# One of a unit's three weight transfers issued by ScalarE instead of SP in the first 24 slots

## The chip, the cores and the metric

The kernel runs on one core of a Trainium2 chip. The core has TensorE (PE; its weight loads are shown as PEld), VectorE (DVE), ScalarE (ACT), GpSimd (POOL) and SyncE (SP). DMAs are issued by an engine's own instruction queue, here SP's and ScalarE's, and carried by 16 DMA engines. The metric is the device time of one execution in microseconds; less is better.

## The reference

An attention block with a threshold, then a feed-forward block with SoLU and a layer norm. All data are float32, except that the weights of the second block arrive as float64.

```python
# q, k, v: (8 batches, 8 heads, 576 rows, 64), tau = 0.02
scores = (q @ k.T) / 8
scores = where(scores >= max(scores) - tau, scores, -1e9)
attn = exp(scores - max(scores))
attn = attn / (sum(attn) + 1e-9)
x = (attn @ v)                      # to (4608 tokens, 512)

h = x @ w_in                        # 512 -> 1024
sm = softmax(h)
solu = h * sm
ln = (solu - mean) / sqrt(var + 1e-6) * g_ln
out = ln @ w_out                    # 1024 -> 512
```

## The kernel before

**Slots and units.** The attention is cut into 144 slots, 18 for each of the 8 batches. A slot is 128 rows of scores for each of two heads. In a batch, 16 slots are of kind 0 or 1 (the first 512 of the 576 rows, four pairs of heads) and the last two of kind 2 (the last 64 rows). Two slots in a row, r = 0 and r = 1, make a unit. So units of kind 0 and 1 end at the odd slots 1, 3, ... 15, then 19, 21, ... 33, and so on; slot 17 ends a unit of kind 2.

**What happens to a slot.** The outer loop counts rounds (`rnd`); each round begins one slot. `scores` (L434) multiplies queries and keys on TensorE into two PSUM tiles. `maxes` (L455) takes the row's extreme on VectorE. `ramp` (L470) and `exps` (L479) run on ScalarE, two instructions each. A round later `normalise` (L486, L487, L489) scales the weights `w` on GpSimd, and `blocks` (L501) transposes them on VectorE in blocks of 32 by 32 into the tile T. T holds both slots of a unit, and there are two T buffers.

**The step that the change touches.** The block transposes leave each block at its own 32 partitions. After the second slot of a unit, three DMAs carry T into the tile wT (two buffers), in which the 576 key rows stand on two halves of 64 partitions: one of 576 KB from T's partitions 32 to 95 (L510), and two of 288 KB from partitions 0 to 31 and 96 to 127 (L512). All three are issued by SP, in this order. Units of kind 2 use four smaller ones (L517).

**Who uses wT.** `attend_steps` (L542), three or four rounds after the unit's second slot, multiplies wT with the values on TensorE into pv. Its first instructions read the lower 64 partitions, its later ones the upper. `attended` (L572) copies pv to xh on ScalarE. When the four units of one kind of a batch are done, their tokens go through the feed-forward block: `ff_h` (L605, L595), `ff_max` (L620), `ff_exp` (L629), `ff_mul` (L635), `ff_stats` (L650 to L661), `ff_norm` (L671), `ff_norm2` (L676), `ff_swap` (L687, four DMAs from SP), `ff_turn` (L697), `ff_o` (L710), `ff_out` (L725) and `ff_store` (L738, two DMAs from SP).

**What else runs in the first slots.** In rounds 0 to about 15 the float64 weights are turned into float32, one piece of 128 by 512 a round. SP loads a piece (L251, 512 KB). ScalarE (L263), VectorE (L282, L286, L308) and GpSimd (L332) convert it; pieces of w_out are also scaled by ScalarE (L340). For every other piece of w_out two DMAs from SP (L347, `w<-w`, the tile w2) swap its halves. SP also loads v (L151) and the queries and keys of the next batch (L142, later L168), which TensorE turns (L379) and ScalarE or VectorE copies (L388, L390, L392).

**The order.** The schedule is written by hand: on every engine the instructions stand in the order in which the Python code records them, round after round. In round s + 1, ScalarE's queue has the ramps and exps of slot s + 1, then the copy L572 where a unit is due, and then what `blocks(s)` records for it; after that come `ff_exp`, the weight steps and the next round. Completion of DMAs is counted on eight semaphores, which the DMAs take in turn; a DMA's issue waits until the last one on its semaphore has landed.

Of the kernel before, what the change touches and what calls it, by code (L numbers as in the profile page):

```python
# [20 lines left out]
def kernel(  # L21
# [27 lines left out]
    nc = tc.nc  # L49
# [443 lines left out]
    def blocks(s):  # L493
        b, kind, hp, r = slots[s]
        key = (b, kind, hp)
        if r == 0:
            units[key] = dict(T=work.tile([P, NB, 2, 2, 32], F32, tag="T", name="T"))
        u = units[key]
        T = u["T"]
        for h, w in enumerate(live.pop(s)["w"]):  # L500
            nc.vector.transpose(out=T[:, :, r, h, :], in_=w)  # L501
        if r == 0:
            return


        T = T.rearrange("p (c m) r h x -> p c (m r h x)", c=2)
        u["wT"] = wT = work.tile([P, 2, NK, 2, 2, 32], F32, tag="wT", bufs=2, name="wT")
        to = wT.rearrange("p g m r h x -> p g (m r h x)")
        if kind < 2:
            nc.sync.dma_start(out=to[:, 1], in_=T[32:96])  # L510
            for half in range(2):
                nc.sync.dma_start(out=to[ROWS[half], 0], in_=T[96 * half : 96 * half + 32])  # L512
            return
        for g in range(2):
            for half in range(2):
                of = 64 * half + 32 * g
                nc.sync.dma_start(out=to[ROWS[half], g], in_=T[of : of + 32])  # L517
# [291 lines left out]
    with tc.manual_schedule():  # L809
# [45 lines left out]
        while True:  # L855
# [133 lines left out]
            if rnd - 1 in live:  # L989
                blocks(rnd - 1)  # L990
# [62 lines left out]
```

## Time and profile before

| | us |
|---|---|
| time, median of 3 runs | 857.37 |
| lowest and highest of the 3 | 852.65, 860.28 |
| span of the profiled execution | 854.9 |
| TensorE busy in it | 819.9 |
| VectorE, ScalarE, GpSimd busy | 674.6, 570.0, 496.1 |

The three runs are other executions than the profiled one, whose span, from the first to the last instruction, lies between the lowest and the median of them.

How rows of a timeline read: start in us, length in us, engine, line, operation, out<-in, how many were merged, and in brackets how long the engine was idle ahead of it and what ended that. SPq and ACTq are the instruction queues of SP and ScalarE: a row of theirs is the issuing of a DMA, and the transfer itself lands later. The name `w` stands for three tiles in the profile, since buffer numbers are left out: the attention weights w, and the feed-forward weights w1 and w2.

### The profile page before, as it was taken

Reading aid. Unit: us, or ns where it says so; the run is one execution under the profiler, and the core shown is the slowest. Engines: PE = TensorE matmul, PEld = TensorE weight load, DVE = VectorE, ACT = ScalarE, POOL = GpSimd, SP = SyncE. Lnnn points to the kernel's source line nnn. Section 1 sums busy time; section 2 is a strip of 40 time slices with the busy share of each in tenths; the row PEclk is TensorE's granted clock in tenths of the full one; section 3 lists DMA queues with packets and bytes.
Section 4 is the critical chain, followed back from the end, with each engine's and each line's share of the span. In section 5 each row is a group of like instructions: output and inputs, shape, how many; then the busy total and the mean of one; then the engine's idle time right before and its main releaser. Section 6 shows DMA issues by size and latency. Waiting matters only on the chain.

```text
span 854.9 us, 36109 instructions
## 1 busy us (share of the span) xinstructions
PE 819.9 (96%) x15363; PEld 620.5 (73%) x15363; DVE 674.6 (79%) x1225; ACT 570.0 (67%) x1127; POOL 496.1 (58%) x945
## 2 busy tenths in 40 slices
PE   6778899999999999999999999999999999999997
PEld 5555677778677787777688877777777777777655
DVE  5997787989788888888788878888888878787361
ACT  6886876777767666667666666666677777775121
POOL 4885656666566656565566666565666655555120
PEclk8899999999999999999999999999999999999999
DMA  9999778798888888887888778887788887655212
GB/s 343 254 249 213 191 194 233 188 259 204 226 229 202 211 185 218 216 216 190 201 215 218 195 177 209 207 217 207 195 221 226 207 188 175 165 137 140 67 38 63
DMA packets 75314, 168.54 MB, mean 197 GB/s; under 512 B 11146, under 2 KB 32658, under 8 KB 75154
## 3 DMA queue, kind: packets, MB, share of 16 engines
q1 hardware_dynamic: 74866, 165.82, 76.7%
q8 instruction: 120, 1.97, 1.0%
q10 hardware_dynamic: 288, 0.43, 0.2%
q14 instruction: 40, 0.33, 0.1%
HBM read 46.14 MB, written 9.44 MB: 65 GB/s over the span
## 4 chain that ended last, share of the span: by engine, by line
PE 83%; DMA 4%; DVE 4%; ACT 3%; issue 2%; POOL 2%; SPq 1%; DVEq 0%; ACTq 0%; POOLq 0%
PE o_ps L710 27%; PE h_ps L605 22%; PE s_ps L434 15%; PE pv L542 14%; DMA wT<-T 3%; PE h_ps L595 3%; ACT w L470 1%; DVE w L455 1%; ACT w L479 1%; DVE T L501 1%; POOL w L489 1%; POOL sm L487 0%; PE s_ps L379 0%; DVE w L308 0%; PE tp L371 0%
## 5 line engine op out<-in xcount | busy, mean ns | idle before, releaser
L710 PE MATMUL o_ps<-w,uT 64*64 64x256 f32 x4608 | 269.5, 376 | 2.2 <-issue 1.6
L470 ACT ACTIVATE w<-s_ps,nth 128x576 f32<-128x576 f32 x280 | 196.8, 738 | 105.6 <-DVE nth L455 88.6
L455 DVE CUSTOM_DVE_ANT_0 w<-s_ps,tau_t 128x576 f32<-128x576 f32 x280 | 200.0, 751 | 83.5 <-PE s_ps L434 52.4
L710 PEld LDWEIGHTS o_ps<-w,uT 64*64 64x64 f32 x4608 | 221.8, 133 | 55.4 <-ACT xh L572 12.0
L489 POOL TENSOR_SCALAR w<-w,sm 128x576 f32<-128x576 f32 x288 | 220.6, 778 | 14.3
L501 DVE STREAM_TRANSPOSE T<-w 128x576 f32<-128x576 f32 x288 | 207.7, 756 | 22.6 <-POOL w L489 22.3
L605 PE MATMUL h_ps<-w,xh 64*64 64x512 f32 x1856 | 220.8, 589 | 0.0
L479 ACT ACTIVATE w<-w,ntau 128x576 f32<-128x576 f32 x288 | 219.6, 767 | 0.0
L542 PEld LDWEIGHTS pv<-wT,v 64*64 64x64 f32 x5760 | 172.6, 136 | 39.8 <-issue 16.7
L434 PE MATMUL s_ps<-kT,qT 64*64 64x512 f32 (+1 forms) x2048 | 175.8, 416 | 13.4 <-ACT w L470 11.3
L542 PE MATMUL pv<-wT,v 64*64 64x128 f32 (+1 forms) x5760 | 173.9, 263 | 8.3 <-DMA wT<-T 7.4
L605 PEld LDWEIGHTS h_ps<-w,xh 64*64 64x64 f32 x1856 | 118.4, 133 | 77.2 <-issue 43.6
L486 POOL TENSOR_SCALAR sm<-sm 128x2 f32<-128x2 f32 x144 | 34.2, 237 | 186.5 <-ACT w L479 182.8
L487 POOL TENSOR_TENSOR sm<-sm,mone 128x2 f32<-128x2 f32 x144 | 106.7, 741 | 12.0
L434 PEld LDWEIGHTS s_ps<-kT,qT 64*64 64x64 f32 x2048 | 72.7, 137 | 21.7 <-ACT w L470 16.2
L572 ACT COPY xh<-pv 128x256 f32<-128x256 f32 x64 | 25.4, 396 | 80.9 <-PE pv L542 80.9
L671 ACT ACTIVATE V<-u,nb,rs 128x1024 f32<-128x1024 f32 x36 | 44.7, 1240 | 40.5 <-POOL nb L661 33.6
L697 DVE STREAM_TRANSPOSE uT<-V 128x1024 f32<-128x1024 f32 x36 | 44.1, 1225 | 15.9 <-DMA V<-u 15.6
L479 ACT ACTIVATION_READ_ACCUMULATOR w<-w,ntau 128x1 f32 x288 | 55.4, 192 | 0.0
L676 DVE TENSOR_SCALAR u<-u,rs,nb 128x1024 f32<-128x1024 f32 x36 | 34.9, 971 | 19.5 <-ACT V L671 17.9
L635 DVE TENSOR_TENSOR u<-h_ps,u 128x1024 f32<-128x1024 f32 x36 | 42.8, 1190 | 9.4 <-ACT u L629 9.4
L620 DVE TENSOR_REDUCE hm<-h_ps 128x1 f32<-128x1024 f32 x36 | 42.9, 1193 | 4.9 <-PE h_ps L595 2.7
(77 smaller groups left out, 553.5 us busy)
## 6 DMA issues: line engine op xcount, KB each, us to landing
wT<-T SPq DMA_DIRECT2D x160, 288.0 KB, 6.5
wT<-T SPq DMA_DIRECT2D x64, 576.0 KB, 5.5
v<-in_v_dram SPq DMA_DIRECT2D x16, 576.0 KB, 6.0
V<-u SPq DMA_DIRECT2D x144, 64.0 KB, 3.5
out_dram<-ob SPq DMA_DIRECT2D x71, 128.0 KB, 2.6
q<-in_q_dram SPq DMA_DIRECT2D x28, 288.0 KB, 6.1
k<-in_k_dram SPq DMA_DIRECT2D x27, 288.0 KB, 6.4
qT<-flip SPq DMA_DIRECT2D x48, 144.0 KB, 3.2
```

The source lines that it names most:

```text
L434: nc.tensor.matmul(out=ps[h][ROWS[y], ks], lhsT=lhsT, rhs=d["kT"][ROWS[h], ks], start=True, stop=True,)
L455: nc.vector.tensor_tensor_reduce(out=w, in0=ps[:, 0:S], in1=(zero if loose else tau_t).to_broadcast([P, S]), scale=1.0, scalar=BIG, op0=AL ...
L470: nc.scalar.activation(out=d["w"][x], in_=d["w"][x] if d["loose"] else d["ps"][x][:, 0:S], func=AF.Prelu, bias=d["nth"][x], scale=-1.0, al ...
L479: nc.scalar.activation(out=w, in_=w, func=AF.Exp, bias=ntau, scale=1.0, accum_out=sm[:, x : x + 1])
L487: nc.gpsimd.tensor_tensor(out=sm, in0=sm, in1=mone, op=ALU.pow)
L489: nc.gpsimd.tensor_scalar(out=w, in0=w, scalar1=sm[:, x : x + 1], scalar2=1.0, op0=ALU.mult, op1=ALU.mult)
L501: nc.vector.transpose(out=T[:, :, r, h, :], in_=w)
L542: nc.tensor.matmul(out=to, lhsT=d["v"][ROWS[u], (h0 + h - u) % 4, m,], rhs=rhs, start=m == 0, stop=m == NK - 1,)
L605: mm = nc.tensor.matmul(out=h[ROWS[y], f], lhsT=x[ROWS[r], c, ROWS[y]], rhs=w1_parts[ROWS[r], c, part ^ r], start=part == 0 and c == 0, st ...
L671: nc.scalar.activation(out=V, in_=u, func=AF.Identity, bias=nb, scale=rs)
L697: nc.vector.transpose(out=uT, in_=d["V"].rearrange("p y (m x) -> p m y x", x=32))
L710: nc.tensor.matmul(out=d["o"][ROWS[z], 512 * (r ^ other) : 512 * (r ^ other) + 256], lhsT=d["uT"][ROWS[r], m].rearrange("p y x -> p (y x)" ...
```

## The change

One line in `blocks`: for units whose second slot is below 24, the first of the three transfers is issued by ScalarE on its own queue.

```diff
         if kind < 2:
-            nc.sync.dma_start(out=to[:, 1], in_=T[32:96])
+            (nc.scalar if s < 24 else nc.sync).dma_start(out=to[:, 1], in_=T[32:96])
             for half in range(2):
                 nc.sync.dma_start(out=to[ROWS[half], 0], in_=T[96 * half : 96 * half + 32])
             return
```

That is 11 units: those of slots 1, 3, 5, 7, 9, 11, 13, 15, 19, 21 and 23. The other 53 units of these kinds, and those of kind 2, stay as they were. The turn in which DMAs take the eight semaphores changes with it. In order of instructions, ScalarE's issue stands directly behind the two exps of the following slot (slots 5, 7, 13, 19 and 21 of those), behind copies of queries and keys (slots 1 and 3), or behind the copy L572 (slots 9, 11, 15 and 23). In the first slots the weight step L263 follows it, otherwise L340, L629 or the next ramp.

## The prediction

> **What bounds the kernel now.** I read the page first: busy shares by engine and by slice.
>
> ```profile
> PE 819.9 (96%) x15363; PEld 620.5 (73%) x15363; DVE 674.6 (79%) x1225; ACT 570.0 (67%) x1127; POOL 496.1 (58%) x945
> ...
> PE   6778899999999999999999999999999999999997
> ...
> DMA  9999778798888888887888778887788887655212
> ```
>
> TensorE is full everywhere but in the first slices, and a slice is 854.9 / 40 = 21.4 us. The change ends at slot 23, so I cut the span by stages (columns: stretch, its length, busy us and instructions of PE, PEld, DVE, ACT, POOL, granted clock, DMA share, GB/s).
>
> ```profile
> 55.00:60.00 5.00, 2.19 (x52) 1.36 (x48) 4.83 (x10) 4.98 (x12) 4.65 (x8) 1.00 0.85 227
> ...
> 65.00:70.00 5.00, 4.86 (x54) 2.70 (x45) 4.33 (x10) 4.76 (x10) 4.20 (x8) 1.00 1.04 213
> 70.00:75.00 5.00, 1.84 (x40) 1.60 (x44) 3.44 (x4) 0.12 (x2) 4.36 (x7) 0.92 1.06 228
> ...
> 180.00:400.00 220.00, 219.53 (x4232) 168.21 (x4228) 185.23 (x336) 153.90 (x306) 135.87 (x263) 1.00 0.85 213
> ```
>
> From 180 us on TensorE idles 0.47 us in 220: nothing to be won or lost there unless something new breaks it. From 65 to 75 us the 16 DMA engines are at 1.04 and 1.06 of their time, and TensorE is busy 1.84 of the 5 us from 70 on. Next I read the chain of waits in order of time (start, us, what) and then TensorE's and VectorE's timelines at the same place, for what each idle gap ended on.
>
> ```profile
> 58.08 1.51 DVE T L501 x2
> ...
> 61.22 12.33 DMA wT<-T
> ```
>
> ```profile
> 57.71 0.44 PE L542 MATMUL pv<-wT,v 64*64 64x128 f32 x4 [2.10 <-DMA wT<-T]
> ...
> 72.10 0.44 PE L542 MATMUL pv<-wT,v 64*64 64x128 f32 x4 [2.24 <-DMA wT<-T]
> 73.59 3.36 PE L542 MATMUL pv<-wT,v 64*64 64x128 f32 x66 [1.06 <-DMA wT<-T]
> ```
>
> ```profile
> 78.37 0.76 DVE L455 CUSTOM_DVE_ANT_0 w<-s_ps,tau_t 128x576 f32<-128x576 f32 x1 [4.86 <-PE s_ps L434]
> ```
>
> The longest piece of the chain before the full stretch is one unit's wT, the unit of slot 9 (I count units from 0, so it is unit 4): its T is complete at 58.08 + 1.51 = 59.59, and its last half is there at about 73.55. TensorE loses 2.24 + 1.06 = 3.30 us there and VectorE 4.86. Unit 3 costs TensorE 2.10 at 57.71, beside VectorE's full 4.83 of 5 us. So 3.3 us, at most VectorE's 4.86, is what this change can win at the main place. That is under 1% (8.6 us), about what a measurement here can tell from no change: the three runs alone spread over 7.6 us.
>
> **What SP does with the three transfers.** First the sizes, from the page's list of DMA issues (KB each, median us to landing), then SP's timeline for units 3 and 4 (start, time on the queue), the two half-block issues of unit 3 by themselves (shortest, median, longest ns), and from SP's list of waits what L347 waited for (us in total, times, longest).
>
> ```profile
> wT<-T SPq DMA_DIRECT2D x160, 288.0 KB, 6.5
> wT<-T SPq DMA_DIRECT2D x64, 576.0 KB, 5.5
> ```
>
> ```profile
> 50.40 0.58 SPq L510 DMA_DIRECT2D wT<-T  x1
> 51.03 4.00 SPq L512 DMA_DIRECT2D wT<-T  x2
> 55.12 1.81 SPq L251 DMA_DIRECT2D raw<-in_moe_w_out_dram  x2
> 57.35 1.31 SPq L347 DMA_DIRECT2D w<-w  x2
> 59.64 0.58 SPq L510 DMA_DIRECT2D wT<-T  x1
> ...
> 70.75 1.98 SPq L347 DMA_DIRECT2D w<-w  x2
> ```
>
> ```profile
> L512 SPq DMA_DIRECT2D wT<-T x2: 598/1972/3345, 51.0 to 51.7; - x2
> ```
>
> ```profile
> SPq L347 <- ACT w L340: 4.2, 3, 3.6
> ...
> SPq L347 <- DMA wT<-T: 2.4, 2, 1.7
> ```
>
> The first issue of a unit takes 0.58 us, the second 0.60, the third 3.35: SP is held there, and the weight loads (L251) behind it start only at 55.12. The change takes the large first transfer (576 KB; the halves are 288 KB) off this queue. Both halves move up 0.58 + 0.05 us. If the third issue is held because the large one is in front of it, SP also wins 3.35 - 0.60 = 2.75 us, and L251 would start at about 51.7 instead of 55.12. The w swaps (L347) do not follow: they wait for ScalarE's L340 anyway. What the early weight loads buy is the unused part of 55 to 60, (1 - 0.85) x 5 = 0.75 us of all DMA engines, and perhaps as much again from what the tail behind it no longer drags. I take 1.5 us earlier for unit 4's last half (72.0 instead of 73.5), between 0 (the engines are full, the same bytes must go through) and 3.3 (all of TensorE's hole). A loss is possible too, down to the 1.5 us by which ScalarE issues unit 4's transfer later (below). The Trainium skill, DMA: Bandwidth & Descriptors, section "Issuing engines are not separate DMA queues", says that DMAs from all issuing engines run on the same 16 DMA engines, and that issuing from several saves only the time to initiate, usually small beside the transfer. By that rule alone the gain would be the 0.58 us per unit; the trace agrees on the full engines (1.04 and 1.06) and not on "small", with 3.35 us of issue in one place.
>
> **What ScalarE pays.** The issue takes about 0.6 us of its queue, 11 times (slots 1 to 15, 19, 21, 23). It stands behind the next slot's ramp (L470) and exp (L479), so it can go out later than on SP, and whatever follows on ScalarE (weight step L263 or L340, then the next ramp, which TensorE's next scores and GpSimd's next normalise wait for) is held while it waits. Does 0.6 us cost anything? ScalarE's queue works ahead of its engine:
>
> ```profile
> L263 ACTq EVENT_SEMAPHORE  x1: 17/17/17, 23.1 to 23.1; - x1
> L263 ACT ACTIVATE em<-raw x1: 679/679/679, 24.1 to 24.1; 128x512 int32<-128x512 uint32 x1
> ```
>
> ```profile
> 25.03 1.42 ACT L470 ACTIVATE w<-s_ps,nth 128x576 f32<-128x576 f32 x2 [0.20 <-DVE nth L455]
> ...
> 43.78 1.42 ACT L470 ACTIVATE w<-s_ps,nth 128x576 f32<-128x576 f32 x2 [1.64 <-DVE nth L455]
> ```
>
> The queue handled L263's wait at 23.1 while its engine came to L263 at 24.1, one microsecond later, and it is just there, ahead of L263, that unit 0's issue is put. So 0.6 us is covered by what the engine still has to do. On top there is idle time before the ramps, 0.20 us here and 1.64 in another round. I take 0 for ten of the issues; without that cover it would be 11 x 0.6 = 6.6 us less the idle time.
>
> Unit 4 is later: its place is behind the copy L572, which itself waits for unit 3's attention.
>
> ```profile
> 61.09 0.41 ACT L572 COPY xh<-pv 128x256 f32<-128x256 f32 x1 [0.83 <-PE pv L542]
> ```
>
> So it goes out at about 61.1, 1.5 us after 59.64. It does not come last for that: on a queue of its own it has nothing in front of it, while the halves stand behind two weight loads and two w swaps.
>
> **Unit 5 is the one that costs.** Each DMA of the program takes the next of eight completion semaphores, and its issue waits until the DMA eight before it has landed (that is why SP's L347, which neither reads nor writes wT, waited twice for a wT in the list of waits above). In the changed program ScalarE's transfer of unit 5 (slot 11) shares its semaphore with the first of the two w swaps that SP issues at 70.75 now, and that swap shares one with a half of unit 4. The swap's own issue and landing, and ScalarE's timeline around it:
>
> ```profile
> L347 SPq DMA_DIRECT2D w<-w x1: 653/653/653, 70.7 to 70.7; - x1
> ...
> DMA to landing us min/median/max: 8.1/8.1/8.1
> ```
>
> ```profile
> 77.20 0.39 ACT L572 COPY xh<-pv 128x256 f32<-128x256 f32 x1 [7.09 <-PE pv L542]
> 77.48 1.12 ACT L629 ACTIVATE u<-h_ps,hm 128x1024 f32<-128x1024 f32 x1
> ...
> 79.75 1.37 ACT L470 ACTIVATE w<-s_ps,nth 128x576 f32<-128x576 f32 x2
> ```
>
> It lands at 70.7 + 8.1 = 78.8. ScalarE reaches the new issue behind L572, at 77.3 now, and L629 and the ramp at 79.75 stand behind it. With everything 1.5 us earlier the swap lands at 77.3; then L629 starts at 77.3 + 0.6 = 77.9 instead of 77.48, and the ramp ends at 79.75 + 1.37 + 0.4 = 81.5 instead of 81.1. TensorE, 1.5 us ahead by then, meets that ramp at its next scores and gives back about 1 of its 1.5 us. No other unit meets such a pair: by the program's list of waits, their semaphores were last used by transfers long landed.
>
> **The sum:** SP's relief -1.5, ten hidden issues 0, the hold at unit 5 +1.0: -0.5 us. On the profiled span that is 854.4. The runs' median is 2.5 us above that span (857.37 to 854.9), so 856.9 us.
>
> **The rivals.**
> First, no gain in DMA (15 in 100). The bytes ahead of unit 4's last half are the same and the engines are full, so it lands at 73.5 still, the swap at 78.8, and ScalarE is held from 77.3 to 78.8 plus 0.6 of issue: L629 2.0 us late, of which TensorE sees about 1. Time 858.5. For it speaks the DMA share of 1.04 and 1.06; against it SP's 3.35 us hold and the 0.85 of 55 to 60. In this case the change does not do what moving a transfer seems to promise, since the halves still come last.
>
> Second, the gain is kept (20 in 100). If unit 4's halves land by 70, the swap lands by 75.5, before ScalarE comes to it; TensorE's hole of 3.3 us closes, VectorE's 4.86 with it, and unit 3's hole gives some tenths. -3.3 to -4.9, so 852.5 to 854. For it: two queues with mixed traffic may use the engines better than one. Against it: at 65 to 70 they moved only 213 GB/s at a share of 1.04, so each transfer is slow for another reason than the queue.
>
> Third, slower (15 in 100): ScalarE's issue is held as SP's third one is, because the two halves go out just ahead of it. Price: 2.5 to 3.35 us per issue, of which 1.0 is covered by the queue's lead and 0.20 to 1.64 by idle time. For the five units up to 60 us, on the chain that ends in unit 4's T, that is 5 x (2.9 - 1.0 - 0.6) = 6.5 us, and units 7 and on add up to 1.5. Time 862 to 866. It decides from an issue of 1.0 + 0.6 = 1.6 us on. The trace has just one pair issued by both engines at once:
>
> ```profile
> 851.22 0.72 ACTq L738 DMA_DIRECT2D out_dram<-ob  x1
> ```
>
> ```profile
> 851.22 0.59 SPq L738 DMA_DIRECT2D out_dram<-ob  x1
> ```
>
> ScalarE's took 0.13 us longer than SP's, which speaks against a hold, though neither had a large one beside it. The same page of the Trainium skill, section "Queues, rings and completion order", says that SP and ACT each own a ring on every DMA engine but no descriptor generator of their own; were that what holds SP's third issue, this rival follows, and the pair of 0.72 and 0.59 does not show it.
>
> **How the numbers follow.** The forecast, -0.5 with 50 in 100, has its own range of -2 to +2, so 855 to 859. The rivals give 858.5, 853 and 864. The median of a few runs moves by some 3 us by itself. Leaving out the ends of the second and third case, 8 in 10 lie in 850 to 864. Faster by over 1% (under 848.8) needs more than every wT hole together, so only the scatter of runs could show it: 0.03. Slower by over 1% (over 865.9) is the upper end of the third rival, or several holds like unit 5's that I did not see: 0.09. Within 1%: 0.88.
>
> **What would show it.** SP's third issue of a unit (now the second half) at 0.6 us and L251 of unit 3 near 51.7: relief right. ScalarE's L510 at 0.6 us with no later ramp: hidden. ScalarE idle ahead of L629 in unit 5, ended by the landing of w<-w: the hold. TensorE's two wT holes at 72 and 73.6 smaller by 1.5 in sum, and the stretch from 180 us on as long as before. The forecast is wrong if ScalarE's issues take over 1.6 us, if a wT hole turns up at a unit that has none now, or if the stretch behind 180 us changes.

## The result, and the profile after

| | median us | runs | lowest to highest |
|---|---|---|---|
| before | 855.06 | 20 | 852.48 to 861.56 |
| after | 861.11 | 20 | 855.80 to 865.07 |

The ratio is 1.0053, 95% interval 1.0029 to 1.0076: about 4.5 us of 855.06 lost (the two medians lie 6.05 us apart, the two means 4.70). The forecast was a gain of 0.5 us and a time of 855 to 859 us. The profiled execution after has a span of 857.8 us.

In what follows a hole is a stretch in which TensorE is idle, and the head is the first 85 us or so, in which the DMA engines are nearly always busy and units 0 to 5 are moved.

The same stages as before (stretch, its length, busy us and instructions of PE, PEld, DVE, ACT, POOL, granted clock, DMA share, GB/s):

```profile
50.00:55.00 5.00, 2.52 (x32) 1.43 (x28) 4.51 (x10) 4.39 (x11) 4.40 (x7) 0.56 1.04 238
55.00:60.00 5.00, 3.76 (x72) 2.87 (x64) 3.11 (x7) 2.85 (x7) 4.18 (x8) 0.76 1.03 263
60.00:65.00 5.00, 0.89 (x8) 0.52 (x12) 2.93 (x7) 2.44 (x6) 2.42 (x5) 0.58 1.04 260
...
70.00:75.00 5.00, 5.00 (x58) 3.21 (x54) 4.81 (x12) 4.91 (x10) 1.89 (x5) 1.00 0.87 218
180.00:400.00 220.00, 217.99 (x4144) 162.14 (x4140) 182.74 (x335) 152.85 (x303) 134.09 (x260) 1.00 0.84 210
```

TensorE, which idled from 70 to 75 before, is full there now. The idle stretch has moved forward: 0.89 us of work between 60 and 65, at a granted clock of 0.58. The DMA engines are full in these 15 us (1.03 to 1.04). The stretch from 180 on idles 2.01 us instead of 0.47. SP's, TensorE's and ScalarE's timelines after show what moved:

```profile
50.31 1.72 SPq L512 DMA_DIRECT2D wT<-T  x2
52.68 3.10 SPq L251 DMA_DIRECT2D raw<-in_moe_w_out_dram  x2
```

```profile
52.71 0.69 PE L542 MATMUL pv<-wT,v 64*64 64x128 f32 x4 [1.95 <-DMA wT<-T]
53.92 3.75 PE L542 MATMUL pv<-wT,v 64*64 64x128 f32 x66 [0.52 <-DMA wT<-T]
...
63.73 0.69 PE L542 MATMUL pv<-wT,v 64*64 64x128 f32 x4 [4.98 <-DMA wT<-T]
64.80 3.44 PE L542 MATMUL pv<-wT,v 64*64 64x128 f32 x66 [0.38 <-DMA wT<-T]
...
76.79 2.23 PE L542 MATMUL pv<-wT,v 64*64 64x128 f32 x70
```

```profile
68.39 0.39 ACT L572 COPY xh<-pv 128x256 f32<-128x256 f32 x1 [5.96 <-PE pv L542]
68.55 0.55 ACTq L510 DMA_DIRECT2D wT<-T  x1
...
79.31 0.55 ACTq L510 DMA_DIRECT2D wT<-T  x1
79.91 1.11 ACT L629 ACTIVATE u<-h_ps,hm 128x1024 f32<-128x1024 f32 x1 [0.34 <-issue]
```

SP is relieved: its two half-block issues take 0.54 us each, and L251 starts at 52.68 instead of 55.12. But unit 3's halves now take over 13 us to land; of the two, the profile before shows the landing of the second alone, 7.14 us after its issue (SP's L512 issues of unit 3 by themselves, shortest, median, longest):

```profile
DMA to landing us min/median/max: 13.1/13.2/13.3
```

So the holes are at units 2 (1.95 + 0.52) and 3 (4.98 + 0.38), and unit 4 has none. The page's list of DMA issues has the large transfers at 5.4 us to landing on SP's queue and 8.3 on ScalarE's (median). These are not the same transfers: the eleven are issued in the first 150 us, the 53 behind them. On SP, in both profiles of the kernel before, the eleven have a median of 6.7 us (landings are known for five and six of them, for eight on ScalarE). So the queue accounts for some 1.6 us of the difference, and the place for the rest.

```profile
wT<-T SPq DMA_DIRECT2D x53, 576.0 KB, 5.4
...
wT<-T ACTq DMA_DIRECT2D x11, 576.0 KB, 8.3
```

### The profile page after: what moved, and what is told of

Read it like the earlier page. It is cut to its first block, busy times and chain, and to the rows that moved or that the text cites. A ratio compares the mean times of both kernels' runs of the same rounds, so it can differ in the third digit from the quotient of the medians.

```text
span 857.8 us, 36130 instructions
## 1 busy us (share of the span) xinstructions
PE 819.2 (95%) x15363; PEld 617.1 (72%) x15363; DVE 674.6 (79%) x1225; ACT 570.5 (67%) x1127; POOL 494.3 (58%) x945
## 4 chain that ended last, share of the span: by engine, by line
PE 79%; DMA 7%; DVE 4%; ACT 3%; SPq 3%; POOL 2%; issue 2%; ACTq 0%; DVEq 0%; POOLq 0%
PE o_ps L710 25%; PE h_ps L605 22%; PE s_ps L434 14%; PE pv L542 14%; PE h_ps L595 3%; DMA wT<-T 3%; DVE w L455 1%; DMA v<-in_v_dram 1%; DMA q<-in_q_dram 1%; ACT w L479 1%; ACT w L470 1%; DMA raw<-in_moe_w_out_dram 1%; DVE T L501 1%; POOL w L489 1%; SPq L687 1%
## 5 line engine op out<-in xcount | busy, mean ns | idle before, releaser
L710 PE MATMUL o_ps<-w,uT 64*64 64x256 f32 x4608 | 267.9, 376 | 2.0 <-issue 1.4
L710 PEld LDWEIGHTS o_ps<-w,uT 64*64 64x64 f32 x4608 | 229.6, 133 | 48.2 <-issue 13.2
L542 PEld LDWEIGHTS pv<-wT,v 64*64 64x64 f32 x5760 | 169.9, 136 | 43.4 <-issue 23.7
L434 PE MATMUL s_ps<-kT,qT 64*64 64x64 f32 (+1 forms) x2048 | 172.1, 414 | 14.3 <-ACT w L470 11.6
L605 PEld LDWEIGHTS h_ps<-w,xh 64*64 64x64 f32 x1856 | 112.2, 133 | 83.8 <-issue 61.2
L434 PEld LDWEIGHTS s_ps<-kT,qT 64*64 64x64 f32 x2048 | 69.7, 136 | 22.2 <-ACT w L470 16.6
L572 ACT COPY xh<-pv 128x256 f32<-128x256 f32 x64 | 25.6, 399 | 80.3 <-PE pv L542 80.2
L629 ACT ACTIVATE u<-h_ps,hm 128x1024 f32<-128x1024 f32 x36 | 40.2, 1116 | 10.7 <-DMA V<-u 5.7
```

Of the source, the lines that this page charges most:

```text
L434: nc.tensor.matmul(out=ps[h][ROWS[y], ks], lhsT=lhsT, rhs=d["kT"][ROWS[h], ks], start=True, stop=True,)
L542: nc.tensor.matmul(out=to, lhsT=d["v"][ROWS[u], (h0 + h - u) % 4, m,], rhs=rhs, start=m == 0, stop=m == NK - 1,)
L605: mm = nc.tensor.matmul(out=h[ROWS[y], f], lhsT=x[ROWS[r], c, ROWS[y]], rhs=w1_parts[ROWS[r], c, part ^ r], start=part == 0 and c == 0, st ...
L710: nc.tensor.matmul(out=d["o"][ROWS[z], 512 * (r ^ other) : 512 * (r ^ other) + 256], lhsT=d["uT"][ROWS[r], m].rearrange("p y x -> p (y x)" ...
```

## The experiments

The kernels come in four groups. Where only the condition for ScalarE's queue changes, the diff is that one line.

**Which transfers, and which property of them?** Three theories: the two queues make the last part land late (A), ScalarE's late issues at units 4, 5 and 7 hold what follows (B), or the order of the parts matters (C).

```diff
-            (nc.scalar if s < 24 else nc.sync).dma_start(out=to[:, 1], in_=T[32:96])
+            (nc.scalar if s < 8 else nc.sync).dma_start(out=to[:, 1], in_=T[32:96])
```

> ScalarE issues the large transfer of units 0 to 3 only (slots 1 to 7). Theory A (two queues: the halves of a unit stand in SP's queue between weight loads and no longer come with their large transfer, so the last part of a unit lands later; in the profile of after unit 3's halves took 13.05 and 13.27 us to land against 7.14 for the second one before): the loss is made here, ratio 1.003 to 1.006, TensorE's hole at unit 3 near 5 us. Theory B (ScalarE's issues of units 4, 5 and 7 stand behind the copy L572 and hold what follows): nothing of it is left, ratio 0.998 to 1.002, unit 3's hole near 2 us.

Measured: 857.25 us, ratio 1.0019 (0.9992 to 1.0047). Less than the whole, and not told apart from nothing. Unit 3's hole is 1.22 + 1.05 = 2.27 us, nearer to what theory B had.

```diff
-            (nc.scalar if s < 24 else nc.sync).dma_start(out=to[:, 1], in_=T[32:96])
+            (nc.scalar if 8 <= s < 24 else nc.sync).dma_start(out=to[:, 1], in_=T[32:96])
```

> ScalarE issues the large transfer of units 4 and on only (slots 9 to 23). Theory A: the stage up to unit 3 is as before, ratio 0.997 to 1.002; unit 4 may lose up to 2 us. Theory B: the loss is made here, ratio 1.003 to 1.006, with ScalarE idle ahead of L263 or L629 in units 4 and 5.

Measured: 859.99 us, ratio 1.0042 (1.0014 to 1.0071). Against theory A as it was put, with the first four as the only place.

```diff
             for half in range(2):
-                nc.sync.dma_start(out=to[ROWS[half], 0], in_=T[96 * half : 96 * half + 32])
+                (nc.scalar if s < 24 else nc.sync).dma_start(out=to[ROWS[half], 0], in_=T[96 * half : 96 * half + 32])
```

> All three transfers of a unit go by ScalarE's queue up to slot 23. Theory A: the unit is together again and has no weight load in front of it, so its last part lands in 6 to 8 us, the holes at units 3 and 4 go, ratio 0.993 to 0.998. Theory B: ScalarE has three issues where it had one and its third may be held some 3 us as SP's was: ratio 1.006 to 1.015. The third issue's length on ScalarE also tells whether SP's 3.35 us came from the large transfer ahead on the same queue.

Measured: 875.9 us, ratio 1.0228 (1.0199 to 1.0256). ScalarE's queue, on its timeline:

```profile
34.71 0.58 ACTq L510 DMA_DIRECT2D wT<-T  x1
35.33 3.17 ACTq L512 DMA_DIRECT2D wT<-T  x2
```

The two halves of unit 1 take 3.17 us together, as they do on SP before (3.10). So the hold is not SP's own: it moves with the transfers to the queue that issues them. On ScalarE it delays the ramps, which SP has none of: the one behind these issues starts at 39.11 us, before at 34.60. TensorE's holes on wT in units 2 to 4 are gone in this kernel, as theory A had it, but the time is lost ahead of them.

```diff
         if kind < 2:
+            for half in range(2) if s < 24 else ():
+                nc.sync.dma_start(out=to[ROWS[half], 0], in_=T[96 * half : 96 * half + 32])
             nc.sync.dma_start(out=to[:, 1], in_=T[32:96])
-            for half in range(2):
+            for half in range(2) if s >= 24 else ():
```

> Everything stays on SP, but up to slot 23 the halves are issued ahead of the large transfer, as they go out in the changed kernel. Theory A and theory B: no second queue, ratio 0.998 to 1.002. Theory C (it is the order that costs, since the large one comes last, or the shifted turn of the semaphores): ratio 1.003 to 1.006.

Measured: 856.14 us, ratio 1.0005 (0.9986 to 1.0024). The order of the parts alone is not it; theory C falls.

**ScalarE's late issues, and smaller sets of units.** The first of these changes the order on ScalarE alone: up to round 24 the issue stands ahead of the copy L572.

```diff
+                if rnd <= 24 and rnd - 1 in live:
+                    blocks(rnd - 1)
                 attended(attending)
```

> All eleven transfers stay on ScalarE's queue as in the changed kernel, but up to round 24 the issue of a round stands ahead of that round's copy of the finished unit (L572) on ScalarE, so that the issues of units 4 and 5 no longer wait for the pv matmuls of the unit before. Theory B (the issue is late because it is queued behind that copy: 68.55 us in the changed kernel against 59.64 us on SP before): unit 4's issue comes between 60 and 65 us, unit 4's last part lands before 72 us, and the time goes back to 855 to 857.5 us (ratio at most 1.002). Theory A (two queues share the engines, and the last part lands later whichever moment ScalarE issues): the issue is early but the time stays at 858.5 to 861 us (ratio 1.004 to 1.006).

Measured: 861.14 us, ratio 1.0048 (1.0030 to 1.0067). ScalarE's queue and TensorE, on their timelines:

```profile
59.30 0.55 ACTq L510 DMA_DIRECT2D wT<-T  x1
```

```profile
59.80 0.69 PE L542 MATMUL pv<-wT,v 64*64 64x128 f32 x4 [4.86 <-DMA wT<-T]
```

Unit 4's issue is 9 us earlier than in the changed kernel, unit 3's hole is nearly the same (4.86, there 4.98), and the time too. Theory B falls.

```diff
-            (nc.scalar if s < 24 else nc.sync).dma_start(out=to[:, 1], in_=T[32:96])
+            (nc.scalar if 8 <= s < 12 else nc.sync).dma_start(out=to[:, 1], in_=T[32:96])
```

> Only the two large transfers that are queued behind the copy at L572 in the head (units 4 and 5) go to ScalarE's queue; the other nine stay on SP. Theory B: all of the loss is here, 858.5 to 861 us (ratio 1.003 to 1.006), with unit 4's issue near 64 us against 59.64 and the ramp of round 11 later by 3 to 4 us. Theory A: two of eleven, at most 857 us (ratio at most 1.0015).

Measured: 856.87 us, ratio 1.0006 (0.9980 to 1.0031). The two late issues alone cost nothing that can be measured.

```diff
-            (nc.scalar if s < 24 else nc.sync).dma_start(out=to[:, 1], in_=T[32:96])
+            (nc.scalar if 12 <= s < 24 else nc.sync).dma_start(out=to[:, 1], in_=T[32:96])
```

> Only the large transfers of slots 13 to 23 go to ScalarE's queue, five of the eleven; units 0 to 5 stay on SP. Theory B: only one of the five stands behind the copy at L572, and it is past the head: 855 to 857 us (ratio 0.9995 to 1.0015). Theory A: the loss follows the number of transfers on the second queue where the DMA engines are full, so 856 to 858 us. If the loss is made behind the head after all (later landings of 8 to 11 us at 122 to 146 us): 859 us or more.

Measured: 856.95 us, ratio 0.9982 (0.9952 to 1.0011). The five behind the head cost nothing that can be measured. This leaves the later seven unexplained: they are these five and units 4 and 5, and lost 0.42% where the two parts by themselves lose nothing that can be measured. Their profile has a hole of 4.58 us in units 2 and 3, which that kernel leaves on SP.

**The same kernels a second time.**

> The kernel before, with nothing changed, profiled and timed a second time. Ratio 0.998 to 1.002. Theory D (the waits behind the head that no line of the change touches, on the load of q at round 33 and on TensorE's own code at 230 us, differ from execution to execution, and give back or add what the head won): rounds 33 to 44 stand 1 to 4 us away from the first profile of the same kernel. Otherwise every round up to 48 stands within 0.5 us of the first profile.

Measured: ratio 0.9987 (0.9965 to 1.0010), as it should be. Its profile differs from the first one of the same kernel by more than the whole effect: round 16's first ramp starts 3.12 us earlier and round 40's 4.80. Unit 3 and unit 4 on TensorE's timeline of this second profile:

```profile
59.43 0.44 PE L542 MATMUL pv<-wT,v 64*64 64x128 f32 x4 [1.52 <-DMA wT<-T]
60.52 3.69 PE L542 MATMUL pv<-wT,v 64*64 64x128 f32 x66 [0.66 <-DMA wT<-T]
...
72.76 2.23 PE L542 MATMUL pv<-wT,v 64*64 64x128 f32 x70
```

The holes of 2.24 and 1.06 us at unit 4, around which the prediction is built, are not here. From 180 to 400 us this unchanged kernel is busy for less of the time too:

```profile
180.00:400.00 220.00, 218.10 (x4190) 166.41 (x4186) 183.11 (x334) 152.87 (x303) 135.69 (x263) 1.00 0.83 207
```

1.90 us idle, beside 0.47 in the first profile and 2.01 in the changed kernel. Among the fourteen profiles of the table of holes below, the 0.47 us of this first one is the least; the others have 1.66 to 4.10. So the longer idle time behind 180 us cannot be laid on the change.

> The changed kernel with nothing else, profiled and timed a second time: ratio 1.003 to 1.008 if the first comparison holds. Theory A: again holes on wT in units 2 and 3 of together over 3.2 us (7.83 us in its first profile; 1.06 to 4.58 us in six profiles of kernels that leave units 0 to 3 on SP), and unit 3's pv matmuls end after 63.8 us. Theory D (chance of an execution): holes and ends as with units 0 to 3 on SP, about 2.6 us and 62 us.

Measured: 860.79 us, ratio 1.0062 (1.0033 to 1.0091). The loss is real; the holes of units 2 and 3 are 0.29 and 4.18 us this time, 4.47 together.

**How far it reaches, and its mirror.**

```diff
-            (nc.scalar if s < 24 else nc.sync).dma_start(out=to[:, 1], in_=T[32:96])
+            (nc.scalar if s < 12 else nc.sync).dma_start(out=to[:, 1], in_=T[32:96])
```

> The large transfers of units 0 to 5 (six of the eleven, all that lie in the head) go on ScalarE's queue, the other five stay on SP. Theory A, narrowed to the head (the large transfer no longer stands in line ahead of the loads that SP issues later, but shares the full engines with them; units 2 and 3 land late and TensorE waits): the whole loss, 858.5 to 861.5 us (ratio 1.003 to 1.0065), with TensorE's holes on wT in units 2 and 3 together over 3.2 us. If the loss is spread over all eleven, or made behind unit 5: 856 to 858 us (ratio at most 1.0025).

Measured: 859.29 us, ratio 1.0031 (1.0009 to 1.0052). TensorE at units 2 and 3:

```profile
53.44 3.96 PE L542 MATMUL pv<-wT,v 64*64 64x128 f32 x70 [2.74 <-DMA wT<-T]
...
62.24 1.13 PE L542 MATMUL pv<-wT,v 64*64 64x128 f32 x16 [3.76 <-DMA wT<-T]
```

The six transfers of the head are enough for more than half of the loss, as far as the interval tells, by the same two holes.

```diff
-            (nc.scalar if s < 24 else nc.sync).dma_start(out=to[:, 1], in_=T[32:96])
+            (nc.scalar if s < 200 else nc.sync).dma_start(out=to[:, 1], in_=T[32:96])
```

> All 64 large transfers go on ScalarE's queue, not only the eleven up to slot 23. Theory A, narrowed to the head: behind the head TensorE is busy throughout and the later landing stays hidden, so no more is lost than in the changed kernel, 858.5 to 862.5 us (ratio 1.003 to 1.008). If each transfer on the second queue costs its share (4.6 us over eleven, 0.4 us each): 64 of them, 880 us or more. If it is ScalarE's issue that costs where ScalarE is close behind: 865 to 880 us, with ScalarE's ramps later from round 26 on.

Measured: 860.80 us, ratio 1.0054 (1.0032 to 1.0077). All 64 cost what eleven cost. The price per transfer is there, as the list of DMA issues shows (7.4 us to landing for all 64, where before has 5.5), but behind the head TensorE has other work. This profile's holes at units 2 and 3 are only 2.39 us together, against the rule that the other profiles suggest (below).

```profile
wT<-T ACTq DMA_DIRECT2D x64, 576.0 KB, 7.4
```

```diff
-            (nc.scalar if s < 24 else nc.sync).dma_start(out=to[:, 1], in_=T[32:96])
+            nc.sync.dma_start(out=to[:, 1], in_=T[32:96])
             for half in range(2):
-                nc.sync.dma_start(out=to[ROWS[half], 0], in_=T[96 * half : 96 * half + 32])
+                (nc.scalar if s < 24 else nc.sync).dma_start(out=to[ROWS[half], 0], in_=T[96 * half : 96 * half + 32])
```

> The mirror of the change: up to slot 23 the large transfer stays on SP and the two halves go on ScalarE's queue. Theory A (a part on a second queue shares the engines with what SP issues later): the halves land late in its place, holes in units 2 and 3 over 3.2 us and 858.5 to 861.5 us (ratio 1.003 to 1.0065); ScalarE's second issue costs it 0.6 us more per unit, which units 0 to 3 show as a ramp later by at most 0.6 us. If only the large transfer's place matters (it stays in line here): 855 to 857.5 us.

Measured: 868.94 us, ratio 1.0131 (1.0098 to 1.0164): worse than either theory had it. ScalarE's timeline:

```profile
23.25 0.66 ACTq L512 DMA_DIRECT2D wT<-T  x1
24.02 2.57 ACTq L512 DMA_DIRECT2D wT<-T  x1
27.26 1.35 ACT L470 ACTIVATE w<-s_ps,nth 128x576 f32<-128x576 f32 x2
```

The second issue on ScalarE is held 2.57 us, with only the two halves on that queue, and the ramp behind it starts at 27.26 instead of 25.03. The holes in units 2 and 3 are 2.15 and 1.55 us, over 3.2 together as theory A had it. Part of this kernel's loss is this hold, so as a test of A it is mixed.

**Two queues as such, or SP's earlier loads?** In the six profiles so far in which SP issues all three transfers of unit 3, the first L251 behind them goes out 3.2 to 4.8 us after unit 3's T is complete; in the six with the large one on ScalarE, 1.4 to 2.5 us after it. Theory F blames those earlier loads. Here the weight loads asked for in rounds 4, 6 and 8 are held on SP until ScalarE's second ramp of the next round, once in the changed kernel and once in the kernel before.

```diff
-                ramp(rnd, 1)
+                done = ramp(rnd, 1)
+                for y in held:
+                    sync(weight_load(y), done)
+                held = []
...
                 for y in ASK.get(x, ()):
-                    weight_load(y)
+                    if rnd in (4, 6, 8):
+                        held.append(y)
+                    else:
+                        weight_load(y)
```

> The changed kernel, with the loads of weights that SP asks for in rounds 4, 6 and 8 (units 1, 2 and 3) held on SP until after the second ramp of the next round, which puts their issue at about 36, 45 and 54.5 us, where the kernel before has it, and not at 33, 44.9 and 52.7 us. Theory F (the loads come up earlier and run beside the parts): unit 3's last part lands near 60 us, the holes on wT in units 2 and 3 come to 2.6 us together, and the time goes back to 855 to 858 us (ratio at most 1.0025). Theory A (two queues share the engines in any case): holes over 3.2 us and 858.5 to 861.5 us (ratio 1.003 to 1.0065).

Measured: 859.95 us, ratio 1.0038 (1.0017 to 1.0060).

> The control: the kernel before with the same hold on the same three loads. By both theories nearly nothing moves, since SP's own hold lasts until about then: 855 to 857.5 us (ratio 0.998 to 1.002). If the hold itself makes a load of weights late (a later round's L263 waits for it), the ratio is above 1.003 here, and what the other kernel shows has to be read against this one.

Measured: 854.84 us, ratio 0.9991 (0.9961 to 1.0020). In the first of the two, SP and TensorE show (its lines lie one further down):

```profile
53.55 3.08 SPq L251 DMA_DIRECT2D raw<-in_moe_w_out_dram  x2
```

```profile
59.20 2.04 PE L543 MATMUL pv<-wT,v 64*64 64x128 f32 x28 [3.42 <-DMA wT<-T]
```

The loads go out late again, the control loses nothing, and a hole of 3.42 us and most of the loss stay. The hole alone would not decide, since kernels with everything on SP have up to 4.58 us; the time does. Theory F is unlikely as the main cause; that it has a small share is open, since the interval takes in the full loss as well as a third of it.

**All profiles together.** TensorE's idle time on wT in units 2 and 3, us:

| units 2 and 3 | one value for each profile | mean |
|---|---|---|
| all three parts on SP (before twice, before with loads held, halves first, only units 4 and 5, only the later seven, only slots 13 to 23) | 2.82, 2.79, 2.96, 2.57, 2.03, 4.58, 1.06 | 2.69 |
| large part on ScalarE (after twice, first four, first six, all units, ahead of the copy, loads held) | 7.83, 4.47, 3.26, 6.50, 2.39, 5.27, 3.42 | 4.73 |

The groups overlap, but the second is 2.0 us longer on average: a little under half of the 4.5 us. Unit 4 is not in the table, and it holds 3.30 us in the first profile of the kernel before. With it the means are 3.67 and 5.03 us, and the difference is 1.4. By the start of round 12's first ramp the second group stands 2.7 us behind the first in the mean, by round 16's 1.7, by round 22's 2.0, by round 23's 3.5 and by round 48's 4.7 us.

## Why the prediction was wrong

**The bound: right in kind, but one execution's.** What limits the head is the landing of wT on full DMA engines. That this costs 3.30 us at unit 4 was one execution; the second profile of the same kernel has 2.79 us at units 2 and 3 and none at unit 4. (The prediction's 2.10 us for unit 3 leaves out a second wait of 0.72 us on the same unit.) So "at most VectorE's 4.86" to be won was never a fixed stock.

**SP's relief: it came, and its price was wrong in sign.** At unit 3 the second half's issue fell from 3.35 to 0.54 us and L251 came at 52.68, forecast 51.7. That the large transfer in front was the reason for the hold is not borne out: ScalarE's second issue was held 2.57 us with no large one in its queue. The term of -1.5 us did not come: unit 3's halves landed 13.05 and 13.27 us after issue, where the one known before took 7.14. TensorE began unit 4 at 76.79 us instead of 72.10, and in the group means round 12 stands 2.7 us later, not 1.5 earlier.

**The step that failed** is the one under this term: that the halves land earlier once the large transfer has left their queue, and that this one loses nothing by it, since "on a queue of its own it has nothing in front of it". Nothing stands in front of it in its own line, but it has to share the engines with the other line. The DMA queues from 50 to 56 us, right after unit 3's issues (packets, MB, share of 16 engines), in the kernel before:

```profile
q1 hardware_dynamic: 427, 1.61, 95.2%
```

and in the kernel after, with q10 as ScalarE's queue:

```profile
q1 hardware_dynamic: 323, 1.15, 82.0%
q10 hardware_dynamic: 61, 0.28, 21.5%
```

Before, one line had the engines: first what was ahead, then unit 3's three parts, then the next loads. After, the large transfer gets about a fifth of the engines' time, and has moved 0.28 of its 0.59 MB when 6 us are over. The halves stand in q1 behind loads of weights that the second queue has slowed: the loads issued at 44.86 and 46.32 land 11.23 and 12.87 us later, before it was 7.39 for the second of them. The size was this execution's: in the second profiles of the two kernels the same load takes 10.14 us after and 9.16 before, and unit 3's second half 10.16 and 8.80. The direction is the same in both pairs. The Trainium skill, DMA: Bandwidth & Descriptors, section "Queues, rings and completion order", says that each DMA engine takes turns, packet by packet, between the queues it has work for. That both queues were served in the same 6 us agrees; the shares, 82.0 and 21.5%, are far from equal, and no row here shows single turns. The prediction drew on that section for its rule on rings alone, and on the neighbouring one ("Issuing engines are not separate DMA queues"), by which another issuer saves initiation time and the engines are shared; it had no rival in which the sharing itself costs.

The engines did not carry less for it. From 30 to 66 us, before and after:

```profile
30.00:66.00 36.00, 26.33 (x494) 18.44 (x492) 34.39 (x70) 31.37 (x65) 30.70 (x42) 0.91 0.98 257
```

```profile
30.00:66.00 36.00, 21.36 (x390) 14.62 (x390) 30.09 (x61) 27.03 (x55) 28.58 (x40) 0.78 1.02 258
```

257 and 258 GB/s (the 6 us from 50 to 56 by themselves had less after, 1.43 MB in all instead of 1.62, which the next 8 us made up). More transfers are under way at once, the same bytes arrive, and each transfer takes longer; a unit waits for its last part. That this sharing is the mechanism is argued from these rows, not shown by an experiment that switches it off. That the second queue costs is shown by the changed kernel, twice. That it costs in the head and not behind it is what the first six, all 64 and the five later ones say; the later seven, with 0.42% lost, do not fit, and that stays open.

**What ScalarE pays: right.** The issues took 0.55 to 0.68 us, and the ramps up to round 9 start within 0.18 us of where they did. Rival three (a held issue) did not come up in this kernel. It is real, though: with a second transfer on ScalarE's queue the hold is 2.57 us, and that kernel loses 1.3%.

**Unit 4's later place: wrong size, no matter.** Forecast 1.5 us later than 59.64; it went out at 68.55, since L572 waited for unit 3, and it did come after the one half whose landing is known (75.56 and 71.72). With that place mended the time is the same.

**Unit 5's hold: mis-sized.** The term was +1.0 us; L629 had waited 0.34 us on the issue, since w<-w had landed at 79.17, just ahead of ScalarE's issue at 79.31.

**The stretch behind 180 us** was named as a sign of error. It did change, but it changes in the unchanged kernel too. What stays open is the larger part of the 4.5 us. Of the 2.7 us in the group means at round 12, 1.7 are left at round 16; the other 3 come by round 48, and 1.5 of them in one step, from round 22 to 23. In that step lies the hole of the last section.

## What to carry to other kernels

Here, with the DMA engines full, a second issuing queue moved no more bytes. It turned a line into sharing, and a consumer that needs several transfers got the last one later. Look at the DMA share before moving an issue, and at how many bytes lie ahead in each line. Before building on a hole in one profile, take a second profile of the same kernel: here waits of 3 us moved from one unit to another by themselves.

## What the runs showed of the hardware

**TensorE waits for its own code.** A hole at the same matmul of the program (o_ps, L710, at 123 to 144 us) is in every profile, with the release named "issue". Its length goes from 0.17 to 4.29 us. TensorE in the second profile of the changed kernel, and the DMA queues of its window from 129 to 130.9 us:

```profile
132.32 3.92 PE L710 MATMUL o_ps<-w,uT 64*64 64x256 f32 x44 [4.01 <-issue]
```

```profile
q8 instruction: 1, 0.02, 3.8%
```

One packet of 16384 bytes on the instruction queue runs from 129.69 to 130.84 us, and TensorE goes on 1.48 us later. At this matmul it goes on 1.23 to 1.61 us after the end of such a packet in all sixteen profiles. The Trainium skill, Runtime: NRT & Kernel Launch, section "Instruction fetch mechanics", has engines refill their code in blocks of 16 KiB by DMA, at a cost that is mostly hidden. The block agrees with the packet; the cost is not hidden at this matmul. In the seven profiles whose large transfers of slots 19 to 23, those in flight at this time, are on ScalarE's queue the hole is 1.90 us in the mean (0.43 to 4.01), in the seven that have them on SP 1.03 (0.17 to 1.88); the two kernels with halves on ScalarE are left out. That the second queue delays the code too would explain a part of the rest of the loss. The ranges overlap widely, the first six have 1.88 us with these transfers on SP, and no run tests it.

**A long hole can be paid twice.** The 6 us behind that hole of 4.01 us, and behind the one of 1.59 us at the same place in the first profile of the kernel before:

```profile
132.32:138.32 6.00, 6.00 (x80) 4.13 (x84) 0.29 (x1) 0.00 (x0) 3.16 (x5) 0.72 0.88 230
```

```profile
131.15:137.15 6.00, 6.00 (x111) 5.53 (x113) 3.65 (x8) 2.68 (x6) 1.99 (x4) 1.00 1.05 245
```

The granted clock is 0.72 after the long one, which takes 6 x 0.28 = 1.7 us more: the 51 matmuls from there on take 4.71 us, before 3.03. The length of the hole alone does not decide it. After holes of this kind of 2.39 us and more the clock was 0.72 to 0.78, in six of six; after shorter ones it was mostly 1.00, but 0.76 after one of 1.67 us. Where TensorE waits for ScalarE near 93 us (L379), a hole of 2.00 us was followed by 0.72 with units 4 and 5 alone on ScalarE, and one of 2.01 us by 1.00 with the first six. So the same wait of 2 us can cost nothing more or over a microsecond more. What decides is not shown.
